# Chunked attention and a gated FFN on one core: k, q and v loaded with a cast and turned by DMA, instead of cast and turned on the engines

## The chip, the cores and the metric

The kernel runs on one core of one Trainium2 chip. The metric is the device time of one execution in microseconds (us). Each execution that is over 1.5% above the fastest of its kernel is slow.

A core has five engines that run their own instruction streams in order. PE multiplies matrices, ACT computes exponentials and logarithms and copies, DVE and POOL do elementwise work, and SP here only issues DMAs. Matmul results go to PSUM, of which each of the two kernels takes eight banks. Everything else lives in SBUF.

## The reference, cut to what matters

```python
batch, n_heads, seq, head_dim = (4, 8, 768, 64); n_mem = 8
chunk, left_ctx, right_ctx = (32, 16, 8)
for c in range(nc):                                  # 24 chunks of 32 tokens
    k_full = concat([mem_k, k[..., c_start-16 : c_end+8, :]])   # 8 + at most 56 keys
    v_full = concat([mem_v, v[..., same window, :]])
    a = softmax(q_c @ k_full.T / 8)
    out[:, :, chunk c] = a @ v_full
x = out as [3072 tokens, 512]                        # heads side by side
return (relu(x @ w_gate) * (x @ w_val)) @ w_out      # 512 -> 1536 -> 512
```

All inputs and the output are float32. The kernel computes in float16 with float32 accumulation. Inside an instruction, k and q must stand with the head dimension on the 128 partitions, while they lie in memory with tokens as rows. So they have to be cast and turned.

## The kernel before

The 3072 tokens are worked on in eight blocks of 384 (`NB`). A block has four head pairs (`hp`). For each head pair there is a turn (PE transposes, then DVE copies), scores (PE), three exponentials (ACT), values (PE), `ln` and `rinv` (ACT), and a multiplication that writes `xT`, the input of the FFN (DVE). A block's FFN has 12 units (gate and value matmuls, then `gr` on ACT and `gv` on DVE) and three out units. While PE runs the FFN of block n, the attention of block n+1 is put between the units.

```python
    TB = 384; NQ = 4; QB = 96; BAND = 120; J = 4; HP = 4; NDC = 12
    tps = tile_pool(bufs=1, PSUM)    # 1 bank: the turn
    sps = tile_pool(bufs=1, PSUM)    # 2 banks: scores
    xps = tile_pool(bufs=1, PSUM)    # 2 banks: values (x_ps)
    fps = tile_pool(bufs=3, PSUM)    # 3 banks: FFN
    # ... cut ...
    def stage_t(n, hp, pool=None, tag="kq"):         # the turn
        ps = (pool or tps).tile([128, J * (KR + QR)], F16, tag=tag, name="kq_ps")
        for j in range(J):
            nc.tensor.transpose(kps[:, j], k16s[n][:, hp, j]..., ident[:KR, :KR])
        for j in range(J):
            nc.tensor.transpose(qps[:, j], q16s[n][:, hp, j]..., ident[:QR, :QR])
        nc.vector.tensor_copy(kw[...120 keys of 3 windows...], src)       # kwin
        nc.vector.tensor_copy(kw[...the window at the edge...], ...)      # kwin
        for hh in range(2):
            nc.vector.tensor_copy(qb[s, :, :, hh, :]..., qps[s]...)       # qbd
    # ... cut ...
    def stage_a(n, hp):
        X = xps.tile([128, 2, 512], F32, name="x_ps")
        # ... 8 matmuls of values and of ones (the softmax sums) into X ...
        nc.scalar.activation(ln, X[D:128, :, 0:TB], ACT.Ln, scale=1.0 / 64.0)
        nc.scalar.activation(rinv, ln, ACT.Exp, scale=-1.0, bias=mln64[0:D, :])
        for hh in range(2):
            nc.vector.tensor_tensor(
                out=nat(xT[D * hh:D * hh + D, hp, :]), in0=perm(X[0:D, hh, 0:TB]),
                in1=perm(rinv[:, hh, :]), op=ALU.mult)    # strided: puts tokens in order
    # ... cut ...
    PIECES = {0: [("t", 0)], 2: [("s", 0), ("t", 1)], 4: [("a", 0), ("s", 1), ("t", 2)],
              6: [("a", 1), ("s", 2), ("t", 3)], 8: [("a", 2), ("s", 3)], 10: [("a", 3)]}
    for n in range(NB):
        if n + 2 < NB:
            loads(n + 2)                    # f32, issued by SP
        for u in range(NDC + TB // 128):
            # ffn_unit(n, u) or out_unit(n, u - NDC), then PIECES[u] of block n + 1
            if u == 11 and n + 2 < NB:
                casts(n + 2)                # 12 casts to f16 on POOL
```

k and q are loaded four tokens to a row of 1 KB, because that makes large DMA pieces. The price is that columns come out in the order (token mod 4, token div 4). The multiplication into `xT` undoes this with a strided pattern.

The softmax here doesn't subtract the row's maximum and nothing guards it: scores larger than these inputs give would overflow.

Of the kernel before, what the change touches and what calls it, by code (L numbers as in the profile page):

```python
# [17 lines left out]
def kernel(  # L18
# [28 lines left out]
    J = 4  # L47
# [9 lines left out]
    half = ctx.enter_context(tc.tile_pool(name="half", bufs=2))  # L57
    epool = ctx.enter_context(tc.tile_pool(name="epool", bufs=2))
    rpool = ctx.enter_context(tc.tile_pool(name="rpool", bufs=2))
    xpool = ctx.enter_context(tc.tile_pool(name="xpool", bufs=2))  # L60
    gpool = ctx.enter_context(tc.tile_pool(name="gpool", bufs=2))
    grpool = ctx.enter_context(tc.tile_pool(name="grpool", bufs=3))
    opool = ctx.enter_context(tc.tile_pool(name="opool", bufs=3))

    tps = ctx.enter_context(tc.tile_pool(name="tps", bufs=1, space=bass.MemoryType.PSUM))
    sps = ctx.enter_context(tc.tile_pool(name="sps", bufs=1, space=bass.MemoryType.PSUM))
    xps = ctx.enter_context(tc.tile_pool(name="xps", bufs=1, space=bass.MemoryType.PSUM))
    fps = ctx.enter_context(tc.tile_pool(name="fps", bufs=3, space=bass.MemoryType.PSUM))
# [3 lines left out]
    sp = nc.sync.dma_start  # L72
    pool_dma = nc.gpsimd.dma_start


    ident = const.tile([128, 128], F16, name="ident")
    kwins = [[const.tile([128, NQ, 128], F16, name=f"kwin{p}{i}") for i in range(2)] for p in range(2)]
    qbds = [const.tile([128, NQ, 3, 2, 32], F16, name=f"qbd{i}") for i in range(2)]
    vwins = [const.tile([128, HP, NQ, 2, 128], F16, name=f"vwin{p}") for p in range(2)]
    vsts = [const.tile([128, NQ, H, D], F32, name=f"vst{p}") for p in range(2)]  # L80
    bias = const.tile([128, 3], F32, name="bias")
    mln64 = const.tile([128, 1], F32, name="mln64")
    mem32 = const.tile([128, 2, D], F32, name="mem32")
    mem16 = const.tile([128, 2 * D], F16, name="mem16")
    memT = const.tile([128, 128], F16, name="memT")
# [3 lines left out]


    ksts, qsts, k16s, q16s = {}, {}, {}, {}
    last_dma = {}

    def load_k(n, hps):
        b, p = divmod(n, 2)
        if n not in ksts:
            ksts[n] = stg.tile([KR, H, J * D], F32, name="kst")
        r0 = 0 if p == 0 else S // J - KR
        h0, nh = 2 * hps[0], 2 * len(hps)
        src = bass.AP(tensor=k.tensor, offset=k[b, h0, J * r0, 0].offset,  # L100
                      ap=[[J * D, KR], [S * D, nh], [1, J * D]])
        return sp(ksts[n][:, h0:h0 + nh, :], src)

    def load_q(n, hps):
        b, p = divmod(n, 2)
        if n not in qsts:
            qsts[n] = stg.tile([QR, H, J * D], F32, name="qst")
        h0, nh = 2 * hps[0], 2 * len(hps)
        src = bass.AP(tensor=q.tensor, offset=q[b, h0, TB * p, 0].offset,
                      ap=[[J * D, QR], [S * D, nh], [1, J * D]])  # L110
        return sp(qsts[n][:, h0:h0 + nh, :], src)

    def load_v_edge(n):
        b, p = divmod(n, 2)
        if p == 0:
            src = bass.AP(tensor=v.tensor, offset=v[b, 0, 0, 0].offset,
                          ap=[[D, BAND - 16], [S * D, H], [1, D]])
            return sp(vsts[0][16:BAND, 0], src)
        src = bass.AP(tensor=v.tensor, offset=v[b, 0, S - 112, 0].offset,
                      ap=[[D, 112], [S * D, H], [1, D]])  # L120
        return sp(vsts[1][0:112, NQ - 1], src)

    def load_v_head(n, h):
        b, p = divmod(n, 2)
        q0 = 1 - p
        src = bass.AP(tensor=v.tensor, offset=v[b, h, TB * p + QB * q0 - 16, 0].offset,
                      ap=[[D, BAND], [QB * D, NQ - 1], [1, D]])
        return sp(vsts[p][0:BAND, q0:q0 + NQ - 1, h, :], src)  # L128

    def load_v_mem(n, dma=sp):  # L130
        b, p = divmod(n, 2)
        for i in range(NQ):
            src = bass.AP(tensor=mem_v.tensor, offset=mem_v[b, 0, 0, 0].offset,
                          ap=[[D, NMEM], [NMEM * D, H], [1, D]])
            dma(vsts[p][BAND:128, i], src)
# [4 lines left out]

    def cast_k(n, hp, eng):
        if n not in k16s:
            k16s[n] = half.tile([KR, HP, J, 2, D], F16, name="k16")
        eng(k16s[n][:, hp].rearrange("p j h d -> p h j d"),  # L144
            ksts[n][:, 2 * hp:2 * hp + 2, :].rearrange("p h (j d) -> p h j d", j=J))

    def cast_q(n, hp, eng):
        if n not in q16s:
            q16s[n] = half.tile([QR, HP, J, 2, D], F16, name="q16")
        eng(q16s[n][:, hp].rearrange("p j h d -> p h j d"),  # L150
            qsts[n][:, 2 * hp:2 * hp + 2, :].rearrange("p h (j d) -> p h j d", j=J))

    def cast_v(n, hp, eng):
        p = n % 2
        eng(vwins[p][:, hp, :, :, 0:D], vsts[p][:, :, 2 * hp:2 * hp + 2, :])  # L155


    state = {}
    xTs = {}

    def kwin_of(n, hp):
        return kwins[n % 2][hp % 2]

    def mem_cols(n, hp, eng):
        b = n // 2
        c0 = (b * HP + hp) * NMEM
        src = bass.AP(tensor=memT.tensor, offset=memT[:, c0:c0 + NMEM].offset,
                      ap=[memT.ap[0], [0, NQ], [1, NMEM]])
        eng(kwin_of(n, hp)[:, :, BAND:128], src)  # L169

    def stage_t(n, hp, pool=None, tag="kq"):
        p = n % 2
        ps = (pool or tps).tile([128, J * (KR + QR)], F16, tag=tag, name="kq_ps")
        kps = ps[:, 0:J * KR].rearrange("p (j r) -> p j r", j=J)
        qps = ps[:, J * KR:].rearrange("p (j r) -> p j r", j=J)
        for j in range(J):
            nc.tensor.transpose(kps[:, j], k16s[n][:, hp, j].rearrange("p h d -> p (h d)"), ident[:KR, :KR])  # L177
        for j in range(J):
            nc.tensor.transpose(qps[:, j], q16s[n][:, hp, j].rearrange("p h d -> p (h d)"), ident[:QR, :QR])  # L179
        kw = kwin_of(n, hp)  # L180
        T = BAND // J

        i0, s0 = (1, 20) if p == 0 else (0, 12)
        src = bass.AP(tensor=ps.tensor, offset=kps[:, 0, s0:s0 + 1].offset,
                      ap=[ps.ap[0], [QB // J, NQ - 1], [KR, J], [1, T]])
        nc.vector.tensor_copy(kw[:, i0:i0 + NQ - 1, 0:BAND].rearrange("p i (t j) -> p i j t", j=J), src)  # L186
        if p == 0:
            nc.vector.tensor_copy(kw[:, 0, 16:BAND].rearrange("p (t j) -> p j t", j=J), kps[:, :, 0:T - 4])
        else:
            nc.vector.tensor_copy(kw[:, NQ - 1, 0:112].rearrange("p (t j) -> p j t", j=J), kps[:, :, KR - 28:KR])  # L190
        qb = qbds[hp % 2]
        for hh in range(2):
            s = slice(D * hh, D * hh + D)
            nc.vector.tensor_copy(  # L194
                qb[s, :, :, hh, :].rearrange("p i g (j r) -> p (i g) j r", j=J),
                qps[s].rearrange("p j (g r) -> p g j r", r=8))

    def stage_s(n, hp):
        kw, qb = kwin_of(n, hp), qbds[hp % 2]
        sc = sps.tile([128, 2, 512], F32, name="sc_ps")  # L200
        for i in range(NQ):
            nc.tensor.matmul(sc[:, i // 2, 192 * (i % 2):192 * (i % 2) + 192], lhsT=kw[:, i, :],  # L202
                             rhs=qb[:, i].rearrange("p g h c -> p (g h c)"), start=True, stop=True)
        ex = epool.tile([128, NQ, 3, 2, 32], F16, name="ex")
        for g in range(3):
            src = sc[:, :, 0:2 * 192].rearrange("p a (b g c) -> p a b g c", b=2, g=3)[:, :, :, g, :]
            dst = ex.rearrange("p (a b) g h c -> p a b g (h c)", b=2)[:, :, :, g, :]
            nc.scalar.activation(dst, src, ACT.Exp, scale=SCALE, bias=bias[:, g:g + 1])  # L208
        state[n, hp] = ex
# [6 lines left out]
    def perm(ap):  # L216
        return ap.rearrange("p (g j r) -> p g j r", j=J, r=8)

    def nat(ap):
        return ap.rearrange("p (g r j) -> p g j r", j=J, r=8)  # L220

    def stage_a(n, hp):
        ex = state.pop((n, hp))
        vw = vwins[n % 2]
        X = xps.tile([128, 2, 512], F32, name="x_ps")
        for i in range(NQ):
            for hh in range(2):
                nc.tensor.matmul(X[:, hh, QB * i:QB * i + QB], lhsT=vw[:, hp, i, hh, :],  # L228
                                 rhs=ex[:, i, :, hh, :], start=True, stop=True)
        ln = rpool.tile([D, 2, TB], F32, name="ln")  # L230
        nc.scalar.activation(ln, X[D:128, :, 0:TB], ACT.Ln, scale=1.0 / 64.0)  # L231
        rinv = rpool.tile([D, 2, TB], F32, name="rinv")
        nc.scalar.activation(rinv, ln, ACT.Exp, scale=-1.0, bias=mln64[0:D, :])  # L233
        xT = x_of(n)
        for hh in range(2):
            nc.vector.tensor_tensor(  # L236
                out=nat(xT[D * hh:D * hh + D, hp, :]), in0=perm(X[0:D, hh, 0:TB]),
                in1=perm(rinv[:, hh, :]), op=ALU.mult)

    def stage_a_wide(n, hp):  # L240

        ex = state.pop((n, hp))
        vw = vwins[n % 2]
        X = xps.tile([128, 2, 512], F32, name="x_ps")
        for a in (1, 0):
            for i in range(NQ):
                for hh in range(2):
                    nc.tensor.matmul(X[D * hh:D * hh + D, a, QB * i:QB * i + QB],
                                     lhsT=vw[:, hp, i, hh, D * a:D * a + D],
                                     rhs=ex[:, i, :, hh, :], start=True, stop=True)  # L250
# [4 lines left out]
        nc.vector.tensor_tensor(  # L255
            out=nat(x_of(n)[:, hp, :]), in0=perm(X[:, 0, 0:TB]), in1=perm(rinv), op=ALU.mult)
# [4 lines left out]
    def ffn_unit(n, m):  # L261
        if m == 0:
# [211 lines left out]
```

## Time and profile before

The median is 302.56 us. The profiled execution has a span of 300.8 us.

| what | value | where it is read |
|---|---|---|
| PE busy | 243.5 us, 81% | the page, part 1 |
| DVE, ACT, POOL busy | 57%, 50%, 25% | the page, part 1 |
| one block in steady state | 32.2 us, twice 33.85 us | distance of the out matmuls in the chain |
| of that, PE busy, DVE busy | 28.35 us, 21.15 us | busy time by window |
| `xT` multiplication | 996 ns, 8 per block | groups |

The page opens with the busy time of each engine, its share of the span, and its number of instructions:

```profile
span 300.8 us, 4844 instructions
## 1 busy us (share of the span) xinstructions
PE 243.5 (81%) x1753; PEld 145.6 (48%) x1753; DVE 172.3 (57%) x298; ACT 150.0 (50%) x281; POOL 76.2 (25%) x161
```

The chain that ended last, in order of time (start, duration, what). Shown are only the out matmuls of blocks 1 to 5, which mark the same place in each block:

```profile
103.47 5.58 PE o_ps L280 x25
...
135.68 5.57 PE o_ps L280 x25
...
167.88 5.57 PE o_ps L280 x25
...
201.73 5.57 PE o_ps L280 x25
...
235.58 5.57 PE o_ps L280 x25
```

The busy time of each engine between two such marks. The columns are the window, its length, then busy time and count for PE, PE weight loads, DVE, ACT and POOL, then granted clock, DMA share and GB/s:

```profile
core 0: us, PE busy (x) PEld busy (x) DVE busy (x) ACT busy (x) POOL busy (x), PEclk, DMA share, GB/s
135.68:167.88 32.20, 28.35 (x212) 17.05 (x213) 21.15 (x36) 18.87 (x35) 7.52 (x16) 1.00 0.45 110
```

No engine is full: PE idles 32.20 - 28.35 = 3.85 us. The timeline of this block says where. A line gives start, duration, engine, line of the kernel, instruction, and in brackets the idle time just before it and who ended it:

```profile
152.63 0.81 PE L271 MATMUL v_ps<-xT,wv 128*128 128x384 f16 x4 [0.82 <-ACT gr L274]
...
154.96 0.49 PE L202 MATMUL sc_ps<-qbd,kwin 128*128 128x192 f16 x4 [1.18 <-DVE qbd L194]
...
159.72 0.49 PE L202 MATMUL sc_ps<-qbd,kwin 128*128 128x192 f16 x4 [0.96 <-DVE qbd L194]
...
167.88 3.41 PE L280 MATMUL o_ps<-wo,gv 128*128 128x512 f16 x15 [0.82 <-DVE gv L275]
```

These four waits are 3.78 of the 3.85 us. Three of them wait for DVE, which is only 66% busy in this window. (The fourth wait, of `v_ps` on `gr`, is for a bank: the FFN has three, and the next value matmul needs the one that `gr` still reads.) The long DVE instructions are these (groups: line, engine, operation, shapes, count, busy time and mean ns, idle before and its releaser):

```profile
L236 DVE TENSOR_TENSOR xT<-x_ps,rinv 64x384 f16<-64x384 f32 x56 | 55.8, 996 | 24.7 <-ACT rinv L233 24.3
...
L186 DVE COPY kwin<-kq_ps 128x360 f16<-128x360 f16 x32 | 30.8, 961 | 16.5 <-PE kq_ps L179 15.6
...
L194 DVE COPY qbd<-kq_ps 64x384 f16<-64x384 f16 x64 | 23.4, 365 | 1.0
```

The two blocks of 33.85 us suggest that waiting cost PE twice. Each holds 3.4 us in which the granted clock was 0.5, right after a stretch in which PE was busy for less than half of the time. Here is the first of them, with columns as in the table of windows above:

```profile
183.77:187.18 3.41, 1.40 (x15) 0.79 (x14) 3.30 (x7) 2.52 (x6) 3.41 (x7) 1.00 1.22 192
187.18:190.60 3.42, 3.42 (x19) 2.26 (x20) 3.38 (x5) 2.31 (x5) 1.08 (x2) 0.50 0.20 39
```

Before the steady state lies a start of about 70 us in which inputs and 9.4 MB of weights arrive.

### The profile page before, as it was taken

The page shows a single profiled execution, that of the slowest core. Times are in us where ns is not written, and L with a number is a line of the kernel's source. Part 1 is how long each engine was busy: PE and PEld are TensorE (multiplying, and loading weights), DVE is VectorE, ACT ScalarE, POOL GpSimd, SP SyncE. Part 2 cuts the span into 40 slices and gives each one's busy share as a digit, 9 for nine tenths or more (in the row PEclk, how much of TensorE's full clock was granted, in tenths as well). Part 3 has the DMA queues.
Part 4 walks back from the last instruction along what each step waited for, and adds up shares of the span by engine and source line. Part 5 has one row for each costly group of instructions (what it writes and reads, how often), then busy time and mean ns, then how long its engine had stood idle before and what let it go on. Part 6 is the DMA issues. An engine that isn't in the chain of part 4 may idle for free.

```text
span 300.8 us, 4844 instructions
## 1 busy us (share of the span) xinstructions
PE 243.5 (81%) x1753; PEld 145.6 (48%) x1753; DVE 172.3 (57%) x298; ACT 150.0 (50%) x281; POOL 76.2 (25%) x161
## 2 busy tenths in 40 slices
PE   5443447788978899699978897989978897889994
PEld 4332225453655456444645365545645365545651
DVE  5764133793579537970787377762795367932420
ACT  1154012873478427762578147642758148733321
POOL 7293762630044002700152006300180000000000
PEclk9999996999999999999999999899979999999999
DMA  6999999931690049301970179003940110011002
GB/s 168 225 229 185 184 234 233 188 84 37 195 228 14 0 142 254 74 2 76 260 135 0 68 203 198 3 1 121 265 86 3 63 41 2 0 36 71 0 15 93
DMA packets 58716, 33.22 MB, mean 110 GB/s; under 512 B 34628, under 2 KB 55620, under 8 KB 58692
## 3 DMA queue, kind: packets, MB, share of 16 engines
q1 hardware_dynamic: 50484, 28.12, 39.4%
q0 software_dynamic: 7920, 4.72, 10.7%
q8 instruction: 14, 0.23, 0.3%
q10 hardware_dynamic: 288, 0.07, 0.1%
q14 instruction: 10, 0.08, 0.1%
HBM read 31.33 MB, written 6.29 MB: 125 GB/s over the span
## 4 chain that ended last, share of the span: by engine, by line
PE 50%; ACT 14%; issue 10%; DVE 8%; DMA 7%; SPq 6%; POOL 4%; POOLq 0%; DVEq 0%; ACTq 0%
PE o_ps L280 16%; PE v_ps L271 14%; PE g_ps L267 12%; SPq L128 5%; ACT ln L231 5%; ACT rinv L233 4%; DMA vst<-in_v_dram 4%; ACT ex L208 3%; DMA vst<-in_mem_v_dram 3%; DVE xT L236 2%; PE x_ps L228 2%; PE sc_ps L202 2%; DVE kwin L186 2%; DVE qbd L194 2%; PE kq_ps L177 2%
## 5 line engine op out<-in xcount | busy, mean ns | idle before, releaser
L275 DVE TENSOR_TENSOR gv<-v_ps,gr 128x384 f16<-128x384 f32 x96 | 52.0, 557 | 66.8 <-PE v_ps L271 65.1
L271 PE MATMUL v_ps<-xT,wv 128*128 128x384 f16 x384 | 81.1, 335 | 8.4 <-ACT gr L274 8.1
L267 PE MATMUL g_ps<-xT,wg 128*128 128x384 f16 x384 | 82.2, 338 | 1.2 <-DVE xT L255 1.2
L236 DVE TENSOR_TENSOR xT<-x_ps,rinv 64x384 f16<-64x384 f32 x56 | 55.8, 996 | 24.7 <-ACT rinv L233 24.3
L280 PE MATMUL o_ps<-wo,gv 128*128 128x512 f16 x288 | 64.7, 379 | 5.7 <-DVE gv L275 5.7
L274 ACT ACTIVATE gr<-g_ps 128x384 f16<-128x384 f32 x96 | 46.3, 494 | 46.2 <-PE g_ps L267 30.3
L271 PEld LDWEIGHTS <-wv 128*128 128x128 f16 x384 | 38.5, 100 | 39.2 <-issue 16.5
L208 ACT ACTIVATE ex<-sc_ps,bias 128x256 f16<-128x256 f32 x96 | 38.5, 471 | 25.2 <-PE sc_ps L202 15.1
L267 PEld LDWEIGHTS <-wg 128*128 128x128 f16 x384 | 36.6, 101 | 22.1 <-issue 2.9
L280 PEld LDWEIGHTS <-gv 128*128 128x128 f16 x288 | 27.6, 98 | 40.6 <-DVE gv L275 9.2
L169 POOL COPY kwin<-memT 128x32 f16<-128x32 f16 x32 | 6.4, 214 | 136.9 <-PE sc_ps L202 134.4
L283 ACT COPY o_sb<-o_ps 128x512 f32<-128x512 f32 x24 | 14.0, 585 | 53.0 <-PE o_ps L280 53.0
L186 DVE COPY kwin<-kq_ps 128x360 f16<-128x360 f16 x32 | 30.8, 961 | 16.5 <-PE kq_ps L179 15.6
L202 PE MATMUL sc_ps<-qbd,kwin 128*128 128x192 f16 x128 | 17.8, 267 | 19.3 <-DVE qbd L194 11.2
L231 ACT ACTIVATE ln<-x_ps 64x768 f32<-64x768 f32 x28 | 22.6, 807 | 18.3 <-PE x_ps L228 18.3
L233 ACT ACTIVATE rinv<-ln,mln 64x768 f32<-64x768 f32 x28 | 26.2, 935 | 0.9
L194 DVE COPY qbd<-kq_ps 64x384 f16<-64x384 f16 x64 | 23.4, 365 | 1.0
L177 PE MATMUL kq_ps<-ident,k 112*128 112x112 f16 x128 | 13.2, 233 | 10.7 <-DVE k L144 6.5
L202 PEld LDWEIGHTS <-kwin 128*128 128x128 f16 x128 | 11.0, 104 | 22.1 <-issue 10.6
L150 POOL CAST q<-qst 96x512 f16<-96x512 f32 x32 | 19.5, 611 | 7.7 <-DMA qst<-in_q_dram 7.7
L155 POOL CAST vwin<-vst 128x512 f16<-128x512 f32 x29 | 16.6, 611 | 18.3 <-DMA vst<-in_mem_v_dram 18.3
L144 POOL CAST k<-kst 112x512 f16<-112x512 f32 x28 | 17.1, 611 | 0.1
(49 smaller groups left out, 120.4 us busy)
## 6 DMA issues: line engine op xcount, KB each, us to landing
out_dram<-o_sb SPq DMA_DIRECT2D x24, 256.0 KB
vst<-in_v_dram SPq DMA_DIRECT2D x64, 90.0 KB
kst<-in_k_dram SPq DMA_DIRECT2D x6, 896.0 KB
qst<-in_q_dram SPq DMA_DIRECT2D x6, 768.0 KB
wg<-in_moe_w_gate_dram POOLq DMA_DIRECT2D x6, 256.0 KB, 14.5
wv<-in_moe_w_val_dram POOLq DMA_DIRECT2D x6, 256.0 KB, 15.8
wo<-in_moe_w_out_dram POOLq DMA_DIRECT2D x3, 512.0 KB, 12.6
kst<-in_k_dram SPq DMA_DIRECT2D x4, 224.0 KB
```

The lines of the kernel that those rows point to most:

```text
L186: nc.vector.tensor_copy(kw[:, i0:i0 + NQ - 1, 0:BAND].rearrange("p i (t j) -> p i j t", j=J), src)
L194: nc.vector.tensor_copy(qb[s, :, :, hh, :].rearrange("p i g (j r) -> p (i g) j r", j=J), qps[s].rearrange("p j (g r) -> p g j r", r=8))
L202: nc.tensor.matmul(sc[:, i // 2, 192 * (i % 2):192 * (i % 2) + 192], lhsT=kw[:, i, :], rhs=qb[:, i].rearrange("p g h c -> p (g h c)"), sta ...
L208: nc.scalar.activation(dst, src, ACT.Exp, scale=SCALE, bias=bias[:, g:g + 1])
L231: nc.scalar.activation(ln, X[D:128, :, 0:TB], ACT.Ln, scale=1.0 / 64.0)
L233: nc.scalar.activation(rinv, ln, ACT.Exp, scale=-1.0, bias=mln64[0:D, :])
L236: nc.vector.tensor_tensor(out=nat(xT[D * hh:D * hh + D, hp, :]), in0=perm(X[0:D, hh, 0:TB]), in1=perm(rinv[:, hh, :]), op=ALU.mult)
L267: nc.tensor.matmul(g_ps, lhsT=wg[:, f, 128 * m:128 * m + 128], rhs=xT[:, f, :], start=(f == 0), stop=(f == NFC - 1))
L271: nc.tensor.matmul(v_ps, lhsT=wv[:, f, 128 * m:128 * m + 128], rhs=xT[:, f, :], start=(f == 0), stop=(f == NFC - 1))
L274: nc.scalar.activation(gr, g_ps, ACT.Relu)
L275: nc.vector.tensor_tensor(out=gvs[n][:, m, :], in0=v_ps, in1=gr, op=ALU.mult)
L280: nc.tensor.matmul(o_ps, lhsT=gvs[n][:, m, 128 * t:128 * t + 128], rhs=wo[:, m, :], start=(m == 0), stop=(m == NDC - 1))
```

## The change

The intent has four parts.

1. For blocks 2 to 7, k, q and v are loaded token by token (pieces of 256 bytes) and cast to f16 in flight. Then k and q are turned by DMA transposes from SBUF to SBUF. The PE transposes, the `kwin` and `qbd` copies on DVE and the casts on POOL go away for these blocks. Besides issuing the loads, POOL now spreads the turned q into the block-diagonal `qbd`. The Trainium skill ("DMA: Bandwidth & Descriptors", SWDGE vs HWDGE vs iDMA) says that a cast in a DMA must be issued from GpSimd and a plain DMA transpose from SP or ACT. The kernel follows that.
2. Everything is in token order, so that the `xT` multiplication becomes contiguous. Blocks 0 and 1 still come in rows of four tokens and are turned on PE, but the DVE copies after it put them in order.
3. The turn's PSUM bank goes to the FFN, which gets four banks. The steps of attention are spread: scores, values with `ln`, `rinv`, and the multiplication each stand one FFN unit apart.
4. The attention of block 1 is computed before the main loop, and the FFNs of blocks 0 and 1 are run together, unit by unit.

```diff
-    fps = ctx.enter_context(tc.tile_pool(name="fps", bufs=3, space=bass.MemoryType.PSUM))
+    fps = ctx.enter_context(tc.tile_pool(name="fps", bufs=4, space=bass.MemoryType.PSUM))
+    def load_band(n, src_t, dsts):                     # k or v, f32 -> f16 in flight
+        for i in range(NQ):
+            src = bass.AP(tensor=src_t.tensor, offset=src_t[b, 0, tok, 0].offset,
+                          ap=[[D, m1 - m0], [S * D, H], [1, D]])
+            pool_dma(dsts[p][m0:m1, i, :, 0:D], src)
+    def turn_dma(n):
+        nc.sync.dma_start_transpose(kT.rearrange("p i a m -> p (i a) m"),
+                                    k16s[n % 2].rearrange("p i h d -> p (i h d)"))
+        nc.sync.dma_start_transpose(qTs[n].rearrange("p i a m -> p (i a) m"),
+                                    q16s[n].rearrange("p i h d -> p (i h d)"))
+    def spread_q(n, eng):                              # POOL, two copies of 64 x 1536
         ... cut ...
-            nc.vector.tensor_tensor(
-                out=nat(xT[D * hh:D * hh + D, hp, :]), in0=perm(X[0:D, hh, 0:TB]),
-                in1=perm(rinv[:, hh, :]), op=ALU.mult)
+            nc.vector.tensor_tensor(out=xT[D * hh:D * hh + D, hp, :], in0=X[0:D, hh, 0:TB],
+                                    in1=rinv[:, hh, :], op=ALU.mult)
         ... cut: the start ...
+    ffn_units(0, (0, 1))
+    ... attention of block 1: one_c, turn_pe, step_s, step_wide for its four head pairs ...
+    loads(2); turn_dma(2); loads(3); turn_dma(3)
+    ffn_units(1, (0, 1))
+    for m in range(2, NDC):
+        ffn_units(0, (m,))
+        ffn_units(1, (m,))
+    ... six out units of blocks 0 and 1 with the attention of block 2 between them ...
+    LATER = {}
+    for hp in range(HP):
+        for d, w in enumerate("svem"):                 # scores, values + ln, rinv, multiply
+            LATER.setdefault(3 * hp + d, []).insert(0, (w, hp))
-    for n in range(NB):
+    for n in range(2, NB):
         if n + 2 < NB:
             loads(n + 2)
         ... cut ...
-            if u == 11 and n + 2 < NB:
-                casts(n + 2)
+            if u == 9 and n + 2 < NB:
+                turn_dma(n + 2)
+                spread_q(n + 2, pool_copy)
```

## The prediction

> **What bounds the kernel now.** The busy table gives PE 243.5 us of 300.8 (81%), DVE 57%, ACT 50%, POOL 25%. The span has two parts. In the first 65 us weights and inputs arrive: the table of 10 us windows shows DMA over 1.0 from 10 to 60 us and PE at only 4.1 to 5.9 of each 10 us up to 50 us. Then a steady state: in the chain of waits the out-matmuls of successive blocks start at 103.5, 135.7, 167.9, 201.7, 235.6, 267.8 us, so a block takes 32 to 34 us. Its bare FFN needs 24 groups of 0.65 us plus 36 matmuls of about 0.216 us, 23.4 us. The other 9 us are attention: the chain passes ln (0.82), rinv (0.94), the kwin copy (0.98), xT (0.99), qbd, and three FFN banks let PE run into gr/gv waits.
>
> **Removed.** For blocks 2 to 7: 32 PE transposes per block (groups of four, 0.5 us when isolated), and all kwin/qbd evictions on DVE. For 4 head pairs: 0.961 + 0.43 + 2x0.365 = 2.1 us each, 8.5 us of DVE per block. POOL's k, q, v casts go (12 x 0.61 us per block). xT is now contiguous: 996 ns should fall to about gv's 557 ns (same 384 columns from PSUM), 3.5 us per block. DVE per block falls from about 23 to 11 us. ACT's work stays, 20 us per block, better spread (exp, ln, rinv in separate units), with four banks.
>
> **Added.** POOL-issued casting loads in 256-byte pieces: 10,752 per block instead of about 5,500 packets. In the trace plain 256-byte packets run at up to 884 per us (18 ns per engine); 1 KB casting packets cost about 49 ns of an engine, like plain 1 KB ones. So I estimate 18 to 30 ns, 12 to 20 us of DMA per block. POOL issue was 0.75 us for 512 pieces; about 1.4 us for 960, 17 us per block. Two transposes of 0.5 and 0.4 MB follow. The Trainium skill ("Advanced Engine Details and Errata", X-Bar Transpose) expects 350-400 GB/s, 3 us by estimate; no run here has shown one, and I allow 5 to 12 us. Spreading q costs POOL about 3.5 us.
>
> **Critical path.** Steady block: FFN 23.4 + scores and values about 2.6 = 26, ACT slightly over PE in the 12 units: 27.5 us. The input chain per block (loads, transposes, spread; POOL waits for the last before the next loads) is 24 to 32 us, so it is nearly critical. Start: weights land at about 48 us, wo at 55; blocks 0 and 1 share their FFN until about 72 us. Then PE stalls about 10 us at the first score of block 2, because POOL issues all loads of 2 and 3, at most eight outstanding, before it spreads q of 2. Outs end near 98 us; five blocks of 27.5, last block 23.4, tail 3: 262 span; plus clock loss and some input stall: **272 us**, 80% range **257 to 298**. Chances: faster 0.86, same 0.07, slower 0.07.
>
> **What would show it.** Right: no kwin copies after block 1, xT about 560 ns, out-matmuls 27 to 28 us apart, PE over 88% after 100 us, a PE stall on POOL's qbd near 75 us. Wrong: block spacing over 30 us with PE waiting on qbd/kT (transpose or small pieces slow), or xT still near 1 us.
>
> **What would make it wrong.** Casting 256-byte pieces at over 38 ns, or POOL generating under 350 a us: then loads set the pace and the time reaches 300 or more. Transposes of over 10 us each, or ones that hold up other DMA. More clock throttling with a denser PE (granted clock was 0.976; 0.69 in one window). Better: no stall at block 2, giving about 255.

## The result, and the profile after

The kernel after takes 269.84 us (median of 4 runs, 269.82 to 269.99), against 302.56 us. The ratio is 0.892, with a 95% interval of 0.888 to 0.896. Ratios here are the mean time of one kernel's fast runs over that of the other's of the same rounds, so not quite the ratio of the medians quoted.

The page of the kernel after, part 1:

```profile
span 267.8 us, 4350 instructions
## 1 busy us (share of the span) xinstructions
PE 234.3 (88%) x1592; PEld 137.4 (51%) x1592; DVE 106.5 (40%) x193; ACT 144.3 (54%) x281; POOL 108.9 (41%) x138
```

The chain of the kernel after, again only the out matmuls, of blocks 2 to 5 (here all 36 of a block lie on the chain):

```profile
122.69 7.77 PE o_ps L327 x36
...
150.09 7.77 PE o_ps L327 x36
...
177.51 7.77 PE o_ps L327 x36
...
204.90 7.77 PE o_ps L327 x36
```

Busy time by window between two of these marks:

```profile
150.09:177.51 27.42, 26.81 (x181) 15.47 (x180) 10.82 (x20) 18.18 (x37) 12.05 (x14) 1.00 1.06 110
```

A block takes 27.4 us, of which PE is busy 26.8 us. PE's work fell by 28.35 - 26.81 = 1.5 us per block and its idle time from 3.85 to 0.61 us. So two thirds of the gain per block is waiting that went away, and one third is work. DVE's busy time fell by half. These are the only waits of PE left in a block, and the granted clock stays at 1.00 (timeline of the kernel after):

```profile
165.84 0.50 PE L266 MATMUL x_ps<-ex,vwin 128*128 128x96 f16 x8 [0.20 <-DVE xT L281]
...
170.78 0.50 PE L266 MATMUL x_ps<-ex,vwin 128*128 128x96 f16 x8 [0.20 <-DVE xT L281]
...
175.71 0.50 PE L266 MATMUL x_ps<-ex,vwin 128*128 128x96 f16 x8 [0.20 <-DVE xT L281]
```

The groups that answer to those shown before. `kwin` is gone; `qbd` is now POOL's, and waits for the DMA transpose:

```profile
L235 POOL COPY qbd<-qT 64x1536 f16<-64x1536 f16 x12 | 17.6, 1466 | 59.4 <-DMA qT<-q16n 59.0
...
L281 DVE TENSOR_TENSOR xT<-x_ps,rinv 64x384 f16<-64x384 f32 x48 | 26.3, 547 | 16.3 <-ACT rinv L274 16.0
```

Where did the time come from? The FFN of block 2 starts at 108.88 us before and at 102.82 us after. That is 6 us from the start. From there to the end it takes 191.9 us before and 165.0 us after, which is 27 us from the steady state. Of these, 3.3 us are the two stretches at half clock (33.85 - 32.20 = 1.65 us each).

The start of the kernel after is not smooth. Its timeline between the last FFN matmul of the first stretch and the shared FFN shows PE waiting for one DVE instruction after another while the attention of block 1 goes by (the column x counts instructions merged in a line):

```profile
36.65 0.61 PE L212 MATMUL k_ps<-sel,lk 114*128 114x128 f16 x4 [1.84 <-DVE lk L185]
...
44.44 0.61 PE L212 MATMUL k_ps<-sel,lk 114*128 114x128 f16 x4 [2.47 <-DVE lk L185]
...
51.59 0.85 PE L292 MATMUL x_ps<-ex,vwin 128*64 128x96 f16 x16 [1.82 <-DVE xT L299]
52.38 0.50 PE L317 MATMUL g_ps<-xT,wg 128*128 128x384 f16 x1
...
52.99 0.53 PE L317 MATMUL g_ps<-xT,wg 128*128 128x384 f16 x1
...
57.29 0.81 PE L317 MATMUL g_ps<-xT,wg 128*128 128x384 f16 x4
57.94 0.81 PE L317 MATMUL v_ps<-xT,wv 128*128 128x384 f16 x4
```

From 52.38 us the matmuls come 0.3 us apart (gate, value, gate: 0.61 us for two), and from 57.29 us four of them take 0.65 us. PE ran at half rate until about 56.7 us; the granted clock in the records is 0.5 from 36.2 to 56.7 us. The Trainium skill ("TensorE: Matmul & The Clock Gate", Part 1) says that PE is clocked at half rate after an idle window and gets the full rate after some 3.4 us of sustained work. The trace agrees with the second part: 4.3 us after PE became continuously busy the rate doubled. The 3.4 us before the half rate were not quite idle here: PE was busy for 0.75 us of them.

### The profile page after: what moved, and what is told of

Same layout as the page of the kernel before. It is cut to its first block, busy times and chain, and to the rows that moved or that the text cites. A ratio compares the mean times of both kernels' runs of the same rounds, so it can differ in the third digit from the quotient of the medians.

```text
span 267.8 us, 4350 instructions
## 1 busy us (share of the span) xinstructions
PE 234.3 (88%) x1592; PEld 137.4 (51%) x1592; DVE 106.5 (40%) x193; ACT 144.3 (54%) x281; POOL 108.9 (41%) x138
## 4 chain that ended last, share of the span: by engine, by line
PE 70%; DVE 12%; ACT 7%; DMA 5%; issue 3%; POOL 0%; ACTq 0%; DVEq 0%; SPq 0%
PE g_ps L317 21%; PE v_ps L317 20%; PE o_ps L327 20%; DVE xT L281 6%; PE x_ps L266 4%; DVE gv L322 3%; ACT ex L252 2%; DMA vst<-in_mem_v_dram 2%; DMA wg<-in_moe_w_gate_dram 2%; PE sc_ps L245 1%; PE x_ps L292 1%; ACT rinvw L298 1%; DMA vst<-in_v_dram 1%; PE k_ps L212 1%; DVE xT L299 1%
## 5 line engine op out<-in xcount | busy, mean ns | idle before, releaser
L235 POOL COPY qbd<-qT 64x1536 f16<-64x1536 f16 x12 | 17.6, 1466 | 59.4 <-DMA qT<-q16n 59.0
L281 DVE TENSOR_TENSOR xT<-x_ps,rinv 64x384 f16<-64x384 f32 x48 | 26.3, 547 | 16.3 <-ACT rinv L274 16.0
L151 POOL DMA_DIRECT2D vwin<-in_v_dram x28 | 25.4, 926 | 12.4 <-PE x_ps L266 7.2
L151 POOL DMA_DIRECT2D k<-in_k_dram x24 | 21.5, 907 | 3.1 <-DMA wv<-in_moe_w_val_dram 1.7
L172 POOL DMA_DIRECT2D q16n<-in_q_dram x24 | 18.7, 798 | 7.7 <-DMA wo<-in_moe_w_out_dram 5.6
L212 PE MATMUL k_ps<-sel,lk 118*128 118x128 f16 (+1 forms) x32 | 4.7, 296 | 17.4 <-DVE lk L185 17.4
L245 PE MATMUL sc_ps<-qbd,kT 128*128 128x192 f16 x128 | 18.5, 275 | 1.0 <-ACT ex L252 1.0
L266 PEld LDWEIGHTS <-vwin 128*128 128x128 f16 x192 | 10.1, 97 | 12.3 <-PE v_ps L317 8.4
L266 PE MATMUL x_ps<-ex,vwin 128*128 128x96 f16 x192 | 12.6, 205 | 3.9 <-DVE xT L281 3.0
L245 PEld LDWEIGHTS <-kT 128*128 128x128 f16 x128 | 12.7, 109 | 4.2 <-issue 0.7
```

Source lines behind the costliest of these rows:

```text
L151: pool_dma(dsts[p][m0:m1, i, :, 0:D], src)
L172: pool_dma(q16s[n][:, i], src)
L245: nc.tensor.matmul(sc[:, i // 2, 192 * (i % 2):192 * (i % 2) + 192], lhsT=kT[:, i, hp, :], rhs=qb[:, i, hp].rearrange("p h m -> p (h m)"), ...
L266: nc.tensor.matmul(X[:, hh, QB * i:QB * i + QB], lhsT=vw[:, i, 2 * hp + hh, :], rhs=ex[:, i, hh, :], start=True, stop=True)
L281: nc.vector.tensor_tensor(out=xT[D * hh:D * hh + D, hp, :], in0=X[0:D, hh, 0:TB], in1=rinv[:, hh, :], op=ALU.mult)
```

## The experiments

Twelve kernels were run. First four undo one part of the change each, starting from the kernel after; then the kernel before with one or two parts alone; then the start and the input chain. Each ran in three rounds beside the kernel before, whose medians in these batches were 301.9 to 302.4 us.

### Three FFN banks

```diff
-    fps = ctx.enter_context(tc.tile_pool(name="fps", bufs=4, space=bass.MemoryType.PSUM))
+    fps = ctx.enter_context(tc.tile_pool(name="fps", bufs=3, space=bass.MemoryType.PSUM))
-    ffn_units(0, (0, 1))
+    ffn_units(0, (0,)); ffn_units(0, (1,))        # the same for block 1
```

> The kernel after, with three FFN banks instead of four (and the first two units of a block one after the other). Theory A (PE is kept fed because every other engine has slack and a fourth bank hides the gr wait behind the exponentials): each head pair's exponentials (1.2 us on ACT) now hold back gr, so PE loses 0.5 to 0.8 us four times a block, 2 to 3 us per block, 280 to 288 us. Rival B (banks don't matter once attention is off PE and DVE): under 273 us.

Measured: 271.67 us (271.47 to 271.88), ratio to before 0.899. The steady blocks stay 27.4 us apart; the whole difference of 1.8 us lies before the first out unit (85.40 instead of 83.45 us). Rival B holds. The fourth bank only lets the first two units of blocks 0 and 1 run four accumulations side by side. In the steady state it buys nothing here. Whether it would in the kernel before is another question; see the contiguous `xT` there.

### A strided xT in the kernel after

```diff
+    def scat(ap):
+        return ap.rearrange("p (g r j) -> p g j r", j=J, r=8)
-    nc.vector.tensor_tensor(out=xT[...], in0=X[0:D, hh, 0:TB], in1=rinv[:, hh, :], op=ALU.mult)
+    nc.vector.tensor_tensor(out=scat(xT[...]), in0=scat(X[0:D, hh, 0:TB]), in1=scat(rinv[:, hh, :]), op=ALU.mult)
```

> The kernel after, with the xT multiplication reading and writing with the strided pattern of before (same values, same place). xT should go from 547 ns to about 1 us. Theory A (DVE has slack, 11 us of 27): under 273 us, block spacing under 28 us. Rival C (contiguous xT was on the chain and gave 4 x 2 x 0.45 = 3.6 us per block): 285 to 292 us.

Measured: 286.33 us (285.66 to 286.88), blocks 30.06 us apart, `xT` at 994 ns. Rival C holds, and theory A fails. DVE is busy only 14.40 us of such a block, so it is less than half full, and yet most of the added DVE time comes through: 3.6 us more work, 2.66 us more time. The timeline says why:

```profile
174.47 0.50 PE L266 MATMUL x_ps<-ex,vwin 128*128 128x96 f16 x8 [1.09 <-DVE xT L284]
...
180.30 0.50 PE L266 MATMUL x_ps<-ex,vwin 128*128 128x96 f16 x8 [1.10 <-DVE xT L284]
```

There is one `x_ps` buffer. The values of the next head pair may only be written when the multiplication of the last pair has read it. Between the `rinv` that releases the multiplication and the values of the next pair there is about one unit of PE work, and two multiplications of 1.0 us behind a `gv` of 0.56 us no longer fit into it. With 0.55 us each they fit but for 0.2 us.

### The turn on PE for all blocks

```diff
     def loads(n):
-        load_band(n, k, k16s); load_k_mem(n); load_q_tokens(n)
+        load_k_rows(n, 0, 8); load_k_rows_mem(n); load_q(n, 0, 8)
         load_band(n, v, vwins); load_v_mem(n)
-    STEP = {"s": step_s, ...};  enumerate("svem")
+    STEP = {"t": turn_pe, "s": step_s, ...};  enumerate("tsvem")
-                turn_dma(n + 2); spread_q(n + 2, pool_copy)
+                casts(n + 2)                       # k and q, on POOL
```

> The kernel after, but blocks 2 to 7 turned as blocks 0 and 1 are: k and q loaded as f32, cast on POOL, turned by PE into two FFN banks, moved by DVE. Theory A: PE gets 32 small matmuls (about 1.6 us), DVE 7 us per block, and both share the four banks: 30 to 33 us per block, 285 to 300 us; turning on DMA is the largest single part of the gain. Rival D (order in tokens, banks and the schedule gave the gain, the DMA turn only moved work): under 280 us.

Measured: 292.31 us (291.94 to 292.42), blocks 31.66 us apart. The time lies where theory A put it. In the window of one block PE is busy 29.05 us and DVE 17.28 us, so PE's own work grew by 2.2 us and its idle time by 2.0 us. The idle time is one wait, four times in a block (timeline):

```profile
171.49 0.50 PE L245 MATMUL sc_ps<-qbd,kT 128*128 128x192 f16 x4 [0.65 <-DVE qbd L220]
```

It is the largest of the four single losses: the strided `xT` alone cost 16.5 us, this 22.5 us. But it is more than the loss of the DMA turn. In this variant the scores stand one FFN unit after the turn, where the kernel before has two, and this order is shown below (spread order in the kernel before) to make PE wait for `qbd`. These waits add up to 13.1 us over the run. The turn also borrows two FFN banks. A variant with two units between was not run, so that the turn is the largest single part, as theory A also says, is not shown.

### The steps of attention lumped as before

```diff
-        for d, w in enumerate("svem"):
-            LATER.setdefault(3 * hp + d, []).insert(0, (w, hp))
+        for d, w in ((2, "s"), (4, "vem")):
+            LATER.setdefault(2 * hp + d, [])[0:0] = [(x, hp) for x in w]
```

> The kernel after, with attention in the order of before: values, ln, rinv and the multiplication of a head pair in one FFN unit, together with the next pair's scores, every second unit. Theory A: with four banks and an almost idle DVE this costs 0 to 1 us per block: 270 to 276 us. Rival E (spreading the steps over units is what keeps PE fed): ACT then does 3.0 us in one unit of 1.6 us, PE stalls 1 us four times a block: 285 to 295 us.

Measured: 276.30 us (275.63 to 276.86), blocks 28.77 us apart. It lies at the upper end of what theory A expected and far from rival E; the cost is 1.35 us per block. Its waits are those of PE values on DVE `xT` (10.5 us in all, up to 1.0 us each), the same single buffer. The order is not quite that of before: the edit puts the next pair's scores ahead of the values, so their exponentials (1.2 us on ACT) stand ahead of the `ln` and `rinv` that `xT` needs. How much of the cost is that was not tried.

### The kernel before with a contiguous xT

```diff
-                out=nat(xT[D * hh:D * hh + D, hp, :]), in0=perm(X[0:D, hh, 0:TB]),
-                in1=perm(rinv[:, hh, :]), op=ALU.mult)
+                out=xT[D * hh:D * hh + D, hp, :], in0=X[0:D, hh, 0:TB],
+                in1=rinv[:, hh, :], op=ALU.mult)
```

> The kernel before, with the xT multiplication of blocks 1 to 7 contiguous, as after has it; tokens then come out in the wrong order, so the result is wrong on purpose. Theory F (xT holds the single x_ps buffer and DVE's order, and DVE is 23 us of a 32 us block): about 2 to 4 us per block, 275 to 288 us. Rival G (before is held by the turning evictions and qbd waits, so a shorter xT is absorbed): over 295 us.

Measured: three fast runs of 289.62, 290.53 and 291.56 us, ratio 0.964. This is between the two expectations: 11 us, where 3.6 us per block times seven would be 25. Neither theory had the size right. The trace kept for this run is of a further execution, with a span of 288.1 us. There `xT` takes 550 ns and the blocks come 30.95 us apart, without a stretch at half clock in the steady state. PE waits 2.51 us in a block:

```profile
148.28 0.81 PE L271 MATMUL v_ps<-xT,wv 128*128 128x384 f16 x4 [0.82 <-ACT gr L274]
149.71 0.49 PE L202 MATMUL sc_ps<-qbd,kwin 128*128 128x192 f16 x4 [0.29 <-DVE qbd L194]
...
152.90 0.81 PE L271 MATMUL v_ps<-xT,wv 128*128 128x384 f16 x4 [0.37 <-ACT gr L274]
154.32 0.49 PE L202 MATMUL sc_ps<-qbd,kwin 128*128 128x192 f16 x4 [0.27 <-DVE qbd L194]
...
157.52 0.81 PE L271 MATMUL v_ps<-xT,wv 128*128 128x384 f16 x4 [0.76 <-ACT gr L274]
```

The waits for DVE have nearly gone (2.96 us in the block of before shown above, 0.56 us here), but those for a bank that `gr` still reads grew from 0.82 to 1.95 us. So with three banks these waits take up a part of what the shorter `xT` frees.

The fourth timed execution took 1361 us, with FFN matmuls of 1.38 us instead of 0.34 us, while DVE's and ACT's instructions took as long as ever; it is left out, and its cause is unknown.

The result was meant to be wrong, and was reported correct. Swapping the tokens inside each chunk in the reference's own output changes it by 1.9% in norm, because all tokens of a chunk see the same window with nearly equal weights. A comparison with a tolerance above that does not see this error.

### The kernel before with the spread order, and with both

```diff
-    PIECES = {0: [("t", 0)], 2: [("s", 0), ("t", 1)], ...}
+    for hp in range(HP):
+        for d, w in enumerate("tsaem"):      # turn, scores, values + ln, rinv, multiply
+            PIECES.setdefault(3 * hp + d, []).insert(0, (w, hp))
```

> The kernel before, with only the order of the attention steps changed: turn, scores, values with ln, rinv, and multiplication each one FFN unit apart, as after does (first turn at unit 0, so the last multiplication falls in the second out unit). Theory F: DVE is full where the turn is, so this gives little, 296 to 304 us. Rival E (the spread order itself is a main source): 1.35 us per block, as its removal from after cost, or more: under 293 us.

Measured: 314.04 us (313.62 to 314.07), ratio 1.041. Neither expectation allowed for it: the order that saves 6.5 us in the kernel after costs 12 us in the kernel before. Blocks are 34.2 us apart. In its timeline PE waits for `qbd` four times in a block (0.82 us each) and for `xT` three times (0.72 us each):

```profile
192.12 0.49 PE L202 MATMUL sc_ps<-qbd,kwin 128*128 128x192 f16 x4 [0.82 <-DVE qbd L194]
...
194.63 0.50 PE L228 MATMUL x_ps<-ex,vwin 128*128 128x96 f16 x8 [0.72 <-DVE xT L246]
```

The scores now stand one unit after the turn, where the old order gave two units; the three DVE copies of the turn (2.1 us) do not fit. And the values again wait for the slow `xT`.

> The kernel before with both: the spread order and the contiguous xT (wrong result on purpose). The turn on PE and DVE stays. It should come near the kernel after whose later blocks are turned on PE (292.3 us, 31.7 us per block), less if four shared banks hurt that one: 278 to 292 us under theory F; if the turn is the largest single part, it stays at least 2 us per block, so at least 12 us, above the kernel after, that is over 281 us.

Measured, with the contiguous `xT` as well: three fast runs of 297.65, 298.45 and 299.22 us, ratio 0.990 (its profiled execution was slow; the trace that was kept is of a further one, with a span of 295.6 us). That is above the range of theory F and above the 292.3 us of the kernel after with its turn on PE, but as expected over 281 us. Without the DMA turn, these two parts in this order do not get below the contiguous `xT` alone. In the kept trace the blocks are 32.0 us apart. The waits for `xT` are gone, and the one for `qbd` is left, four times in a block:

```profile
143.75 0.49 PE L202 MATMUL sc_ps<-qbd,kwin 128*128 128x192 f16 x4 [0.81 <-DVE qbd L194]
```

So while the turn is on PE and DVE, the spread order costs time with the slow `xT` (12 us) and with the short one (8 us). With the turn gone and `xT` short it gains. With the turn gone and `xT` slow it was not tried.

### Blocks 0 and 1 fed one after the other

```diff
-    for m in range(2, NDC):
-        ffn_units(0, (m,))
-        ffn_units(1, (m,))
+    for n in range(2):
+        for m in range(2, NDC):
+            ffn_units(n, (m,))
```

> The kernel after, with units 2 to 11 of block 0 run first and then those of block 1, instead of alternating. In the trace all gate and value weights had landed at 45 us, before the shared FFN starts at 52.4 us. Theory H (sharing weights that are already there buys nothing): 269.3 to 270.8 us. Rival I (feeding two blocks together hides the arrival of weights): over 273 us.

Measured: 269.63 us (268.62 to 270.19), against 269.84 us. Theory H holds: when the shared FFN begins, the weights have long arrived, and alternating the two blocks hides nothing.

### Every DMA transpose three times, and twice

```diff
     def turn_dma(n):
+        turn_once(n)
+        turn_once(n)
+        turn_once(n)             # a_turn2: only two
```

> The kernel after, with every DMA transpose issued three times into the same place. q of block 4 is spread at 118 us and first used at about 131 us, and later blocks have some 12 us of slack as well. Theory J (the input chain of loads, transposes and spread is off the critical path): two more pairs of transposes cost 8 to 12 us of that chain and the time stays under 273 us, except for up to 6 us if block 2, which has only 8 us of slack, is late. Rival K (the chain is nearly critical, as the prediction said): 280 us or more.

Measured: 292.93 us (292.67 to 295.96). Theory J fails by 20 us, and rival K holds. Theory J took the 12 us between the spread of q and its use as the room of every block. But the chain is a loop: POOL issues the next block's loads only after it has spread this block's q, and that waits for the transposes. Then the room at the consumer is used up, and after that the loop sets the pace. In the profiled run 11.5 us are lost before the outs of block 2, nothing in the next block, and 3.9 to 5.5 us in each of the three after that. POOL's spreads in this run (POOL timeline) come about 32 us apart, with their waits for the transposes:

```profile
139.80 2.98 POOL L241 COPY qbd<-qT 64x1536 f16<-64x1536 f16 x2 [19.34 <-DMA qT<-q16n]
...
171.22 2.98 POOL L241 COPY qbd<-qT 64x1536 f16<-64x1536 f16 x2 [18.31 <-DMA qT<-q16n]
...
203.90 2.98 POOL L241 COPY qbd<-qT 64x1536 f16<-64x1536 f16 x2 [19.43 <-DMA qT<-q16n]
```

A repeated pair of transposes took about 4.7 us from issue to issue (SP timeline: 127.37 to 132.05 us). So I estimated the loop for one pair at 32 - 2 x 4.7 = 22.6 us (22.7 in the text below), which leaves room for one more pair under PE's 27.4 us, but not for two. That was put to the test:

> The kernel after, with every DMA transpose issued twice instead of three times. With three, blocks came 32 us apart and a repeated pair of transposes took about 4.7 us, so I estimate the loop POOL loads, transposes, spread, next loads at 32 - 2 x 4.7 = 22.7 us for one pair. Theory N (a loop with slack: it sets the pace only where it exceeds PE's 27.4 us): 22.7 + 4.7 = 27.4, so the steady blocks stay at 27.4 to 28.2 us, with a few us lost once at block 2 or 3: 270 to 276 us. Rival O (every extra pair costs in full, half of what three cost): 279 to 283 us.

Measured: 272.25 us (271.1 to 273.39). Theory N holds. The steady blocks are 27.4 us apart (out matmuls at 181.60, 208.99 and 236.39 us), and the 2.4 us are lost once, at the first scores of block 2. One pair more costs nothing per block; two more cost some 5 us per block once the room is used up.

### FFN units of block 0 inside the attention of block 1

```diff
     step_s(1, 0)
+    ffn_units(0, (2,))
     one_c(2); turn_pe(1, 2); step_s(1, 1); step_wide(1, 0)
+    ffn_units(0, (3,))
     one_c(3); turn_pe(1, 3)
+    ffn_units(0, (4,))
     ... and 5, 6, 7, 8 after the next steps; the shared loop leaves them out for block 0 ...
```

> The kernel after, with units 2 to 8 of block 0's FFN put between the attention steps of block 1, where PE is idle about half the time between 33 and 52 us and runs at half clock. Theory L (this stretch waits on DVE and ACT, not on PE or weights): 7 units of 1.3 us leave the shared stretch, and PE warms earlier; attention of block 1 ends 2 to 4 us later; the shared FFN ends at 74 to 78 us instead of 83.3, and the first scores of block 2 then wait for POOL to spread q at 78 us: 262 to 267 us. Rival M (weights arrive too late for these units, or they hold up attention): 268 us or more.

Measured: 263.22 us (262.69 to 264.28), ratio to before 0.873. This version beats both kernels. Theory L holds in its main part. The seven units found room: in the PE timeline the attention's waits are still there, and FFN matmuls stand between them at the full rate.

```profile
46.17 0.40 PE L212 MATMUL k_ps<-sel,lk 114*128 114x128 f16 x4 [1.84 <-DVE lk L185]
46.40 0.34 PE L216 MATMUL q_ps<-ident,lq 96*128 96x96 f16 x4
46.57 0.82 PE L317 MATMUL g_ps<-xT,wg 128*128 128x384 f16 x4
47.23 0.81 PE L317 MATMUL v_ps<-xT,wv 128*128 128x384 f16 x4
...
76.23 2.75 PE L327 MATMUL o_ps<-wo,gv 128*128 128x512 f16 x12
78.82 0.49 PE L245 MATMUL sc_ps<-qbd,kT 128*128 128x192 f16 x4
```

In its records the granted clock is at half only from 36.8 to 40.2 us, 3.4 us instead of 20.5. The shared FFN ends at 76.2 us instead of 83.3. The wait on q of block 2 that I expected next does not come: no idle time stands before the scores at 78.82 us, because POOL had begun to spread q at 72.74 us.

> As the run before, and POOL spreads q of block 2 before it issues the v loads of block 3, not after. If the stall on q of block 2 is there, this takes it away: 1 to 5 us better than the run before, 259 to 265 us. If there is no stall, the same within 0.5 us.

```diff
     load_q_tokens(3)
+    spread_q(2, pool_copy)       # was after the v loads of block 3
     load_band(3, v, vwins)
```

Measured: 263.32 us (three fast runs 262.64 to 263.87; one run of 266.64 us was slow). It is the same as without it, as expected where there is no stall.

## Why the prediction was right, point by point

The total was predicted at 272 us and measured at 269.84 us. The steady state carries this, and the start comes out right only because two errors cancel. There is luck in the sum as well. Its named stages came to a span of 262 us, and 10 us were added for clock loss and input stall. In the trace the start took 4.8 us more than was said and the rest 1.1 us more (102.8 + 165.0 = 267.8 us). The other 2 us lie between the span and the device time, which the prediction did not count. An input stall is not there.

- **Steady block: the time right, its reason in part.** Predicted 27.5 us: 26 us of work on PE, and 1.5 us more because ACT was expected to be slightly over PE in the 12 FFN units. Measured 27.4 us: PE is busy 26.8 us and waits 0.6 us for DVE's `xT`. ACT does not set the pace: it is busy 18.2 us of the block, and no FFN matmul waits for `gr`. So the term for ACT was wrong, and stood in for work on PE that was put too low and for a wait that was not named. DVE was predicted at 11 us per block and measured at 10.8 us; `xT` at 557 ns and measured at 547 ns. The evictions of the turn are gone after block 1.
- **What each part is worth, only partly foreseen.** The prediction listed the removals, but did not say which of them mattered. Undoing one at a time costs 22.5 us (turn), 16.5 us (contiguous `xT`), 6.5 us (spread order) and 1.8 us (fourth bank). These add up to 47 us, more than the whole gain of 33 us, so they are not independent shares; and the first and third of these variants also brought in an order that neither kernel has. Adding them to the kernel before shows the same: the contiguous `xT` alone gains 11 us, the spread order alone loses 12 us. The reason shown for `xT` is the single `x_ps` buffer and DVE's order, not DVE's busy time.
- **Four banks: not needed in the kernel after, open in the kernel before.** The prediction named three banks as a cause of the waits of before. The trace of before bears that out in part: 0.82 of the 3.85 us of waiting in a block are for a bank, and with a contiguous `xT` 1.95 of 2.51 us. In the kernel after, one bank less changes the steady block by nothing. What the fourth bank would do in the kernel before was not tried; its pools already take eight banks.
- **Casting pieces, size off, on the safe side.** Predicted 18 to 30 ns per piece of 256 bytes. Counted from the packet records, 1,166 such pieces start per us between 178 and 180 us, which is 16 / 1,166 = 13.7 ns on each of 16 engines. POOL issues 960 pieces in 0.91 us, where 1.4 us was predicted.
- **Transposes, a little below the range.** Predicted 5 to 12 us for the two. A repeated pair takes about 4.7 us; in the kernel after, the packets of the two take 4.6 to 5.9 us from the first to the last for each of blocks 4 to 7.
- **"The input chain per block is 24 to 32 us, so it is nearly critical": right in kind, a little high.** The estimate from the tripled transposes is 22.6 us, and the doubled ones, which just fit, are consistent with it. The loop then has room of about 5 us, so it does not set the pace of the blocks in this kernel.
- **"Blocks 0 and 1 share their FFN until about 72 us": wrong.** It ended at 83.3 us. The step that failed is the attention of block 1, for which the prediction names no time. Counted back from 72 us by the 22 FFN units of 1.3 us that follow it, it would have ended near 43 us. But it is a chain through DVE and ACT with waits of up to 2.5 us on PE, lasted until 52.4 us, and left PE at half rate until 56.7 us. Filling this stretch with FFN units gave 6.6 us back, which shows that PE had room there; by estimate some 2 us of it are the half rate (half of 4.3 us) that went away.
- **"PE stalls about 10 us at the first score of block 2": wrong.** There is none. POOL began to spread q at 74.95 us, about when I expected it to, but PE came to the scores only at 85.88 us. The two errors were +11 us and -10 us, and the out units ended at 102.8 us instead of 98.

What remains open: the exact share of each part in the 33 us, which the interactions do not allow to be stated; the cause of the 1361 us execution; and how much of the PE-turn variant's loss is its order (one unit between turn and scores) and its two borrowed banks, so whether the turn or the contiguous `xT` is worth more.

## What to carry to other kernels

An engine that is half idle can still set the pace: ask which single buffer its instruction holds and what stands before it in its queue, because shortening a 1 us instruction to 0.55 us was worth 16 us here with that engine at 48%. The worth of a schedule depends on what it schedules; the spread order gained 6.5 us after the turn was gone and lost 12 us while it was there, so try orders again after removing work. And where a chain is a loop (loads wait for a copy that waits for earlier loads), compare its period with the pace of the limiting engine; room at the consumer is spent once.

## What the Trainium skill lacked or had wrong

- "DMA: Bandwidth & Descriptors", Specifications, gives 512 bytes as the least transfer for line rate and says that smaller ones are read-modify-write. In the kernel after, pieces read as 256 bytes and written as 128 bytes with a cast move at 1,166 per us, 298 GB/s of source data (178 to 180 us). Larger casting pieces, the weights, move more in the same trace: pieces of 1 KB at 376 per us (385 GB/s, 42 to 44 us) and of 2 KB at 200 per us (410 GB/s, 36 to 38 us). So the runs agree that small pieces are slower. What the page lacks is a rate for casting in flight.
- "Advanced Engine Details and Errata", X-Bar Transpose (TRN2), expects 350 to 400 GB/s. Transposes between SBUF tiles here stay below that. They move 256-byte packets, in the kernel after at 608 to 774 per us over the two transposes of a block (blocks 4 to 7, 156 to 198 GB/s), at most 832 over 2 us (213 GB/s); where they were issued three times, at 1,018 between 162 and 164 us (261 GB/s). Its other sentence, that transposes are as fast as regular DMAs, roughly holds at this packet size: plain 256-byte packets reached some 850 per us over 2 us in the kernel before.
- "TensorE: Matmul & The Clock Gate", Part 1, agrees with the runs on the warm-up (half rate until 4.3 us after PE became continuously busy). It names an idle window as what brings the half rate; here windows in which PE was busy for part of the time did so too (0.75 of 3.4 us in the kernel after, 1.40 of 3.41 us in the kernel before). For the execution with FFN matmuls of 1.38 us throughout, about four times 0.34 us, the same Part notes that the clock has been seen stuck at a quarter for 50 us and more. The record of that execution lists no throttled clock, so that this was the cause is not shown.
- No page that I read has the issue time of such loads on POOL: 0.91 us for 960 pieces, 0.80 us for 768.
